# Second mixture of experts, slot 0: which engine forms the six low parts of the next slot's first-layer weights

## The chip, the cores and the metric

One core of one Trainium2 chip runs the kernel. The time is the device time of one execution in microseconds (us). Engines: TensorE (PE in the profile, PEld its weight loads), VectorE (DVE), ScalarE (ACT), GpSimd (POOL), SyncE (SP, a DMA queue here). Times inside the profile count from the start of its span.

## The reference, cut to what matters

Three stages follow each other: a linear attention with a delta rule over 768 steps, a bilinear layer, and a mixture of experts that sends each of 3072 tokens to one of 8 experts. The change lies in the third:

```
def _moe2_ref(x, modality_id, w_gate, modality_bias, w1, w2):
    logits = x @ w_gate + modality_bias[modality_id]
    e_idx = np.argmax(logits, axis=1)
    ...
    for e in range(E):
        mask = e_idx == e
        h = np.maximum(x[mask] @ w1[e], 0.0)
        out[mask] = gate_w[mask, None] * (h @ w2[e])
```

Here D = 384 (three blocks of 128 rows, kk = 0 to 2), F = 1024, E = 8, all in float32.

## The kernel before, in words

Every product of float32 matrices is made of three passes on parts: a high part (a copy rounded to fp32r) and a low part (the value less its high part). A weight w1 thus becomes w1h and w1l, and ph = w1h*xh + w1h*xl + w1l*xh.

The experts' stage works in slots of 256 tokens that share an expert (`back`, line 1265), and two half slots. A slot has eight blocks f = 0 to 7 of 128 hidden columns. For each block TensorE writes ph (two PSUM buffers, tag AB, in turn), ScalarE makes hh (the ReLU's high part) from it, and VectorE makes hl from ph and hh; the second layer (`second`) takes them two blocks later into spy or px. The ph of block f can start when the hl of block f - 2 has read its buffer.

Beside its own blocks a slot prepares the next: in each block `ahead(...)` lets the generator `weights` (line 1214) make a number of pieces of the next expert's weights, and `tokens2` (line 1241) transposes the next tokens (spt, sxh, sxl). In slot 0 two pieces are made in each of blocks 0 to 2 and one in each later block. The first six pieces are those of w1: for each kk and each half of 512 columns ScalarE casts the raw tile r to w1h, and then VectorE or GpSimd subtracts to get w1l. In the weights of slot 0 itself (i = 0) VectorE makes all six; in those of the other slots VectorE makes the first W1D = 3 (W1N = 2 halves per kk, so kk = 0 and the first half of kk = 1), GpSimd the other three. The w2 pieces follow: ScalarE casts, VectorE subtracts to w2l. The raw tiles r have five buffers; a load in SP's queue waits until its buffer has been read by both the cast and the subtraction.

Slot 0 also carries the end of the routing (`late`, line 1088, and `place`, line 931), one step per block: in block 1 TensorE counts (pr) and VectorE computes pos, cnt, pos, pf, hi, hi, lo; in block 2 VectorE makes four one-hot tiles (hot); in block 4 TensorE multiplies them (pl) and VectorE adds the result to list. GpSimd's queue starts the stage with two stores of the last token rows (x2d<-xr).

The order of the work on each engine is the order in which the program issues it (a helper chains every instruction behind the one before it on its engine), so an engine never takes a later instruction first. All operations carry the line of that helper, L86, in the profile.

Of the kernel before, what the change touches and what calls it, by code (L numbers as in the profile page):

```python
# [8 lines left out]
F32 = mybir.dt.float32  # L9
# [7 lines left out]
ALU = mybir.AluOpType  # L17
# [50 lines left out]
XGB, W1D, SLAG, W1N = 3, 3, 2, 2  # L68
# [37 lines left out]
class Kernel:  # L106
# [976 lines left out]
    def moe2(self, early, cur):  # L1083
# [26 lines left out]
        def weights():  # L1110

            for j in range(1, len(kinds)):
# [3 lines left out]
                for _ in self.weights(j, todo[j], states[j]):  # L1116
                    self.done = j, self.left
                    yield

        work, self.done = weights(), (0, 0)  # L1120

        def ahead(i):
# [91 lines left out]
    def weights(self, i, fr, st):  # L1214

        nc = self.nc
        wt = self.wset[i % NSET]
        w1h = wt.tile([P, KC, DFF], F32R, tag="w1h", name="w1h")
        w1l = wt.tile([P, KC, DFF], F32R, tag="w1l", name="w1l")
        w2h = wt.tile([P, FC, DM], F32R, tag="w2h", name="w2h")  # L1220
        w2l = wt.tile([P, FC, DM], F32R, tag="w2l", name="w2l")
        st.update(w=(w1h, w1l, w2h, w2l), odd=i % 2)
        self.left = KC * W1N + FC // 2
        for kk in range(KC):
            self.at(100 + i, MIDP + MIDS * 2 * kk / 13)
            r = self.raw()
            for n, g in enumerate(range(0, DFF, DFF // W1N)):
                gs = slice(g, g + DFF // W1N)
                nc.scalar.copy(w1h[:, kk, gs], r[:, gs])
                (nc.vector if i == 0 or kk * W1N + n < W1D else nc.gpsimd).tensor_tensor(out=w1l[:, kk, gs], in0=r[:, gs], in1=w1h[:, kk, gs].bitcast(F32), op=ALU.subtract)  # L1230
                self.left -= 1
                yield
        self.at(100 + i, MIDP + MIDS * 6 / 13)
        for g in range(0, FC, 2):
            r = self.raw()
            nc.scalar.copy(w2h[:, g:g + 2], r)
            nc.vector.tensor_tensor(out=w2l[:, g:g + 2], in0=r, in1=w2h[:, g:g + 2].bitcast(F32), op=ALU.subtract)
            self.left -= 1
            yield
# [159 lines left out]
```

## Time and profile before

| | |
|---|---|
| median of 3 runs | 830.96 us (830.43 to 833.02) |
| the profiled execution | 831.49 us |
| its span | 829.8 us |
| TensorE busy | 783.9 us, 94% |
| VectorE busy | 619.0 us, 75% |
| ScalarE busy | 411.4 us, 50% |
| GpSimd busy | 169.2 us, 20% |
| mean granted TensorE clock | 0.968 of full |

The busy shares are means over all stages, so the place of the change is read by itself: slot 0 of the experts lies between about 580 and 601 us. In a timeline a row gives start, duration, engine, the operation with output and inputs, and in brackets the idle time of the engine before it and what ended it; consecutive equal operations are merged into one row with their count, which then gives the time from the first's start to the last's end. The granted clock is a share of full speed: 1.00 is 2.4 GHz, 0.50 is 1.2 GHz.

### The profile page before, as it was taken

What the parts mean: (1) busy time and instruction counts of PE and PEld (TensorE: products, weight loads), DVE (VectorE), ACT (ScalarE), POOL (GpSimd) and SP (SyncE); (2) the same over time, 40 slices, a digit from 0 to 9 for tenths busy, and PEclk for the clock granted to TensorE, in tenths of its full rate; (3) what the DMA queues carried; (4) which work ended last, traced back from release to release, by engine and by line L of the source; (5) the groups of instructions that cost most, each with busy time, mean ns of one, the idle gap of its engine ahead of it and who ended that gap; (6) DMA issues with size and microseconds to landing.
All of it is one profiled execution on the core that took longest, in us unless ns stands there. A gap on an engine that the chain in (4) does not pass through costs nothing.

```text
span 829.8 us, 23509 instructions
## 1 busy us (share of the span) xinstructions
PE 783.9 (94%) x9519; PEld 727.8 (88%) x9519; DVE 619.0 (75%) x1571; ACT 411.4 (50%) x873; POOL 169.2 (20%) x179
## 2 busy tenths in 40 slices
PE   5797689999999999999999999999999999999994
PEld 5564459899999999999999999999899999999983
DVE  5998878769767977797689864567986777677641
ACT  6366675562536254515552353334555556555541
POOL 4021203100001000010100000003254654645330
PEclk8598889999999999999999999999999999999997
DMA  9953552304121412143112300037556687667610
GB/s 299 299 176 114 159 128 98 85 23 130 44 66 33 123 44 61 39 118 71 36 53 52 102 19 25 21 124 239 172 190 230 219 264 248 220 238 239 215 54 7
DMA packets 71813, 105.35 MB, mean 127 GB/s; under 512 B 33988, under 2 KB 53332, under 8 KB 71696
## 3 DMA queue, kind: packets, MB, share of 16 engines
q1 hardware_dynamic: 64464, 88.35, 34.9%
q0 software_dynamic: 4064, 11.06, 4.0%
q10 hardware_dynamic: 3168, 4.34, 1.5%
q8 instruction: 77, 1.26, 0.7%
q14 instruction: 40, 0.33, 0.1%
HBM read 89.15 MB, written 10.63 MB: 120 GB/s over the span
## 4 chain that ended last, share of the span: by engine, by line
PE 71%; DVE 10%; issue 9%; POOL 4%; ACT 3%; DMA 2%; SPq 0%; POOLq 0%; ACTq 0%; DVEq 0%
PE pAB L86 24%; PE px L86 16%; PE ph L86 8%; PE pkq L86 4%; PE pw L86 3%; PE spy L86 3%; PE py L86 3%; PE pu L86 3%; DVE TT L86 2%; PE pS L86 2%; POOL w1l L86 2%; PE pg L86 2%; DVE tmp L86 2%; DVE Tt L86 1%; PE pf L86 1%
## 5 line engine op out<-in xcount | busy, mean ns | idle before, releaser
L86 PE MATMUL pAB<-x,w 128*128 128x256 f32 x1728 | 229.2, 287 | 0.0
L86 PEld LDWEIGHTS pAB<-x,w 128*128 128x128 f32 x1728 | 214.0, 191 | 4.4
L86 ACT CAST ch<-a 128x256 fp32r<-128x256 f32 x96 | 39.0, 406 | 120.5 <-DVE a L86 120.5
L86 ACT COPY a<-pAB 128x256 f32<-128x256 f32 x96 | 35.7, 372 | 105.2 <-PE pAB L86 97.1
L86 DVE TENSOR_TENSOR a<-a,pAB 128x256 f32<-128x256 f32 x96 | 39.9, 416 | 63.4 <-ACT a L86 62.9
L86 PE MATMUL ph<-sxh,w1h 128*128 128x256 f32 x288 | 82.2, 285 | 1.5 <-DVE hl L86 1.5
L86 PE MATMUL ph<-sxh,w1l 128*128 128x256 f32 x288 | 80.8, 281 | 0.0
L86 PE MATMUL ph<-sxl,w1h 128*128 128x256 f32 x288 | 80.7, 280 | 0.0
L86 ACT ACTIVATE hh<-ph 128x256 fp32r<-128x256 f32 x96 | 37.0, 385 | 86.1 <-PE ph L86 85.7
L86 DVE TENSOR_TENSOR Tt<-tmp,Tt 128x31 f32<-128x31 f32 (+15 forms) x186 | 66.1, 355 | 6.4
L86 DVE TENSOR_TENSOR w2l<-r,w2h 128x768 fp32r<-128x768 f32 x56 | 60.7, 1096 | 11.5 <-ACT w2h L86 11.4
L86 DVE SCALAR_TENSOR_TENSOR hl<-ph,hh 128x256 fp32r<-128x256 f32 x96 | 40.1, 418 | 37.0 <-ACT hh L86 36.6
L86 DVE TENSOR_TENSOR tmp<-Ab,Tt 128x31 f32<-128x31 f32 (+15 forms) x186 | 65.5, 352 | 3.0
L86 PE MATMUL px<-w34h,ch 128*128 128x392 f32 x192 | 65.6, 342 | 0.0
L86 PE MATMUL px<-w34h,cl 128*128 128x392 f32 x192 | 65.5, 341 | 0.0
L86 PE MATMUL px<-w34l,ch 128*128 128x392 f32 x192 | 65.4, 341 | 0.0
L86 POOL TENSOR_TENSOR w1l<-r,w1h 128x512 fp32r<-128x512 f32 x39 | 50.1, 1302 | 46.0 <-ACT w1h L86 45.9
L86 PEld LDWEIGHTS ph<-sxh,w1h 128*128 128x128 f32 x288 | 54.2, 188 | 2.7 <-DVE hl L86 2.5
L86 DVE TENSOR_TENSOR cl<-a,ch 128x256 fp32r<-128x256 f32 x96 | 40.8, 425 | 20.1 <-ACT ch L86 19.3
L86 PEld LDWEIGHTS ph<-sxh,w1l 128*128 128x128 f32 x288 | 54.3, 189 | 0.0
L86 PEld LDWEIGHTS ph<-sxl,w1h 128*128 128x128 f32 x288 | 54.2, 188 | 0.0
L86 ACT CAST w1h<-r 128x512 fp32r<-128x512 f32 x84 | 49.5, 615 | 5.9 <-DMA r<-in_e_w_dram 5.4
(263 smaller groups left out, 1676.1 us busy)
## 6 DMA issues: line engine op xcount, KB each, us to landing
r<-in_e_w_dram SPq DMA_DIRECT2D x42, 512.0 KB, 5.1
r<-in_e_w_dram SPq DMA_DIRECT2D x56, 384.0 KB, 4.2
raw<-in_w_dram SPq DMA_DIRECT2D x25, 512.0 KB, 4.1
kT<-in_kt_dram SPq DMA_DIRECT2D x12, 512.0 KB, 4.8
X<-in_q_dram SPq DMA_DIRECT2D x24, 256.0 KB, 4.5
vt<-in_v_dram SPq DMA_DIRECT2D x12, 384.0 KB, 5.3
kb<-in_kb_dram SPq DMA_DIRECT2D x12, 384.0 KB, 5.0
x2d<-xr ACTq DMA_DIRECT2D x22, 192.5 KB, 2.7
```

What stands on the lines that cost most here:

```text
L86: x = f(*a, **kw)
```

## The change

It alters the choice of engine for w1l in `weights`: the first three pieces go to VectorE only for slots after slot 1 (i > 1). For i = 1, which is prepared in slot 0, all six pieces go to GpSimd. For i = 0 all six stay on VectorE. The subtraction, its operands and the order of issue stay.

```
--- before.py
+++ after.py
@@ -1227,7 +1227,7 @@
             for n, g in enumerate(range(0, DFF, DFF // W1N)):
                 gs = slice(g, g + DFF // W1N)
                 nc.scalar.copy(w1h[:, kk, gs], r[:, gs])
-                (nc.vector if i == 0 or kk * W1N + n < W1D else nc.gpsimd).tensor_tensor(out=w1l[:, kk, gs], in0=r[:, gs], in1=w1h[:, kk, gs].bitcast(F32), op=ALU.subtract)
+                (nc.vector if i == 0 or i > 1 and kk * W1N + n < W1D else nc.gpsimd).tensor_tensor(out=w1l[:, kk, gs], in0=r[:, gs], in1=w1h[:, kk, gs].bitcast(F32), op=ALU.subtract)
                 self.left -= 1
                 yield
```

## Rows read from the trace of the kernel before

**Rows 1.** The page's first line.

```profile
span 829.8 us, 23509 instructions
```

**Rows 2.** Busy time by stretches: each engine's us (instructions), TensorE clock, DMA share, GB/s.

```profile
583.30:590.60 7.30, 5.25 (x38) 4.66 (x35) 7.13 (x17) 5.18 (x13) 5.06 (x6) 1.00 0.60 164
590.60:800.00 209.40, 208.80 (x1473) 206.54 (x1474) 153.52 (x292) 118.04 (x250) 106.04 (x91) 1.00 0.67 220
```

**Rows 3.** Waits of TensorE, 580 to 606: total, times, longest.

```profile
PE ph L86 <- DVE hl L86: 1.5, 2, 1.1
PE spt L86 <- DVE sxl L86: 0.6, 1, 0.6
```

**Rows 4.** Chain of waits in slot 0: start, us, what.

```profile
590.57 1.32 PE ph L86 x9
591.88 0.18 PE pl L86 x2
```

**Rows 5.** Timeline of VectorE in slot 0, and one row of ScalarE's.

```profile
583.67 1.28 DVE L86 TENSOR_TENSOR w1l<-r,w1h 128x512 fp32r<-128x512 f32 x2
584.88 0.42 DVE L86 SCALAR_TENSOR_TENSOR hl<-ph,hh 128x256 fp32r<-128x256 f32 x1
...
585.54 1.78 DVE L86 TENSOR_TENSOR w1l<-r,w1h 128x512 fp32r<-128x512 f32 x1
...
587.52 0.98 DVE L86 TENSOR_TENSOR pos<-pos,oh 128x16 f32<-128x16 f32 x1
...
588.74 1.04 DVE L86 TENSOR_SCALAR hi<-pf 128x2 f32<-128x2 f32 x1
...
590.09 0.42 DVE L86 SCALAR_TENSOR_TENSOR hl<-ph,hh 128x256 fp32r<-128x256 f32 x1
...
583.72 0.38 ACT L86 ACTIVATE hh<-ph 128x256 fp32r<-128x256 f32 x1
```

**Rows 6.** Timeline of GpSimd in slot 0.

```profile
583.95 1.16 POOL L86 DMA_DIRECT2D x2d<-xr  x2 [14.07 <-ACT w1h L86]
585.49 1.28 POOL L86 TENSOR_TENSOR w1l<-r,w1h 128x512 fp32r<-128x512 f32 x1 [0.38 <-ACT w1h L86]
587.12 2.59 POOL L86 TENSOR_TENSOR w1l<-r,w1h 128x512 fp32r<-128x512 f32 x2 [0.36 <-ACT w1h L86]
```

**Rows 7.** VectorE's routing operations by tile: duration in ns, min/median/max; first, last start.

```profile
L86 DVE TENSOR_TENSOR pos<-pos,oh x12: 162/163/980, 185.4 to 587.5; 128x16 f32<-128x16 f32 x12
...
L86 DVE TENSOR_SCALAR hi<-pf x12: 168/170/1036, 185.8 to 588.7; 128x2 f32<-128x2 f32 x12
...
L86 DVE TENSOR_SCALAR hot<-cols,lo,tok x24: 306/308/382, 193.8 to 591.2; 128x128 f16<-128x128 bf16 x24
```

**Rows 8.** Timelines of VectorE and GpSimd in slot 2.

```profile
628.22 3.44 DVE L86 TENSOR_TENSOR w2l<-r,w2h 128x768 fp32r<-128x768 f32 x1 [0.30 <-ACT w2h L86]
...
628.29 2.55 POOL L86 TENSOR_TENSOR w1l<-r,w1h 128x512 fp32r<-128x512 f32 x2
```

**Rows 9.** Busy time by stretches around two idle times of TensorE; columns as in rows 2.

```profile
90.91:97.37 6.46, 0.00 (x1) 0.00 (x0) 6.22 (x11) 2.55 (x6) 3.89 (x6) 0.74 0.44 128
108.99:112.41 3.42, 0.00 (x1) 0.00 (x0) 2.92 (x6) 3.04 (x7) 0.00 (x0) 0.80 0.00 0
112.41:117.87 5.46, 5.46 (x9) 2.93 (x10) 5.03 (x8) 4.19 (x8) 0.00 (x0) 0.50 0.14 27
```

**Rows 10.** Timeline of TensorE behind the second of these idle times.

```profile
112.41 5.59 PE L86 MATMUL pw<-wose,TT 128*128 128x392 f32 x8 [3.42 <-DVE TT L86]
...
118.50 2.14 PE L86 MATMUL pw<-wos,TT 128*128 128x392 f32 x6
```

**Rows 11.** SP's third load of r in slot 0, the landings (575 to 600), the cast.

```profile
589.74 0.35 SPq L86 DMA_DIRECT2D r<-in_e_w_dram  x1
...
DMA to landing us min/median/max: 3.2/3.6/4.1
...
598.73 0.61 ACT L86 CAST w1h<-r 128x512 fp32r<-128x512 f32 x1
```

More of the change, by code (lines that the diff above doesn't have):

```diff
@@ L1229, in weights @@
                 nc.scalar.copy(w1h[:, kk, gs], r[:, gs])
-                (nc.vector if i == 0 or kk * W1N + n < W1D else nc.gpsimd).tensor_tensor(out=w1l[:, kk, gs], in0=r[:, gs], in1=w1h[:, kk, gs].bitcast(F32), op=ALU.subtract)
+                (nc.vector if i == 0 or i > 1 and kk * W1N + n < W1D else nc.gpsimd).tensor_tensor(out=w1l[:, kk, gs], in0=r[:, gs], in1=w1h[:, kk, gs].bitcast(F32), op=ALU.subtract)
                 self.left -= 1
```

## The prediction

> **What bounds the kernel now.** I began with the page: the span is 829.8 us [rows 1]; the execution itself took 831.49, 0.53 above the median of the runs, 830.96, and I add the sum to 831.0. Next, the busy time by stretches: from 590.6 to 800 TensorE works 208.80 of 209.40 us at a granted clock of 1.00, while in the 7.3 us before it works only 5.25 [rows 2]. Thus slot 0 is the one place where this change can meet idle TensorE time, and what slot 0 ends later by, the end gets in full: there are 0.6 us of idle time to absorb it in the next 200. The waits of TensorE there say on whom: ph on VectorE's hl, twice, 1.5 us, the longest 1.1; spt on sxl, 0.6 [rows 3]. The chain of waits enters TensorE from that hl at 590.57, and 1.3 us later comes pl, the product of the hot tiles [rows 4]. (Blocks are f=0 to 7; the late hl is that of f=2, which frees the buffer that the ph of f=4 writes. pl stands behind this ph in TensorE's order, and everything of TensorE stands behind pl.)
>
> VectorE's timeline shows why hl is late [rows 5]: two w1l (1.28 us), hl, sxl, a third w1l that takes 1.78, then routing: pos 0.98, hi 1.04. The medians of these two are 0.163 and 0.170 [rows 7]. GpSimd's timeline beside it: the three long ones end where a GpSimd w1l ends, at about 586.77, 588.5 and 589.7 [rows 6]. So a VectorE operation with two SBUF inputs (w1l, pos), and the tensor_scalar hi, wait while GpSimd runs its subtraction; hl and sxl, which read PSUM, do not. Waiting makes 1.1 + 0.8 + 0.9 = 2.8 us, the work in the w1l 2.0.
>
> **What the change removes.** Three w1l leave VectorE, 1.28 + 1.78 = 3.06 us between the hl of f=0 and pos. Not all comes back: the hl of f=1 needs hh, written by ScalarE from 583.72 to 584.10 [rows 5]. Then hl at 584.15, sxl at 584.5, two short routing operations from 584.8, and the first held one, pos (from pos and oh), asks at about 585.15 and not 587.6. The 0.6 us wait of spt for sxl goes.
>
> **What it adds.** GpSimd has six w1l in a row. Its queue first issues the two x2d stores of the last token rows, 583.95 to 585.11 [rows 6]; by then four of six casts are done, and the fifth was there at 587.12, before its turn. A pair takes 2.59 us, so six take 7.8: GpSimd subtracts without a gap from 585.1 to 592.9, where it did so in three pieces until 589.7. Behind them in its queue stands only the fill of ids, needed much later.
>
> VectorE still has seven operations ahead of pl that I take for held ones: pos, hi, the second hi, four hot. (lo I take as free.) hi and hot are both tensor_scalar with SBUF operands; no row shows hot beside a GpSimd subtraction, its nearest row is hi, held to 1036 ns [rows 7]. The price hangs on who goes first when one GpSimd w1l ends and the next is queued. Two rows differ. pos, waiting since 587.6, got in between the second and third GpSimd w1l [rows 5, 6]. But the w2l at 628.22, queued ahead of the pair that began at 628.29, took 3.44 us: it waited for both and then needed its usual 0.9 [rows 8].
>
> Bounds: if VectorE gets in at every handover, the second hi ends near 589.0, hl (f=2) at 589.5, TensorE begins ph at 589.6, a microsecond early; but four hot then wait for the fourth, fifth and sixth w1l, the last ends at 593.15, and pl comes at 593.2, not 591.9: plus 1.3. If it never gets in, pos starts at 592.9, then pf, hi, hi, lo (four of 0.17) and hl 0.42: ph at 594.0 and not 590.57, plus 3.4; the hot then run beside ph. If hot is never held and every handover is won, TensorE resumes a microsecond early: minus 1.0. With one or two of three handovers won before 592.9, hl begins at about 593.1: plus 2.9. I take that, between the two rows.
>
> **The clock.** TensorE would then stand still from about 589.0 to 593.5, 4.5 us. The traced idle times of 3.42 and 6.46 us, both in the start, have a mean granted clock of 0.80 and 0.74: it fell from 1.00 to 0.50, from 2.4 to 1.2 GHz, 2.1 and 3.1 us into them. Behind the shorter one 5.46 us of work ran at 0.50, so that low stretch was 1.4 + 5.5 = 6.8 us [rows 9]. Eight 128x392 matmuls then take 5.59 us, 0.70 each, and six at full clock 2.14, 0.36 each [rows 10]: about half is lost. An idle time of 4.5 us would leave 4.2 to 5.5 us at low clock behind it, price 2.1 to 2.7; I take 2.3. The floor is nothing (1.1 us of idleness at 590 did not move the clock), the ceiling 3.4, half of 6.8.
>
> **What costs nothing.** The three raw tiles come free about 3 us later (the third at 592.9 and not 589.7), so their next loads do. The third load, issued at 589.74, lands 3.2 to 4.1 us after issue; from 592.9 that is 597.0 at the latest, and ScalarE reads it at 598.73 [rows 11]. Without this cover it would be up to 3 us. SP's queue issues in order, and nothing it holds meanwhile is urgent. Slot 1 reads the last w1l at 601.4, 8 us after it is done.
>
> **Sum:** 831.0 + 2.9 + 2.3 = 836.2 us, 0.6% slower.
>
> **Rivals.**
> A, VectorE gets in at every handover. For: pos; against: w2l. Plus 1.3 without a fall of the clock, 832.3; with one, behind a stall of some 2.4 us, up to 3.2 more, 835.5.
> The Trainium skill's page "SBUF — State Buffer", section "Who interferes with whom", says that whoever issues first gets the shared port pair for its whole instruction and that the other fully blocks. By that rule a VectorE operation already waiting goes ahead of the next GpSimd one, which is A; the pos row agrees and the w2l row does not.
> The page's same section says that a tensor_scalar can take both ports, so hot would be held: by it the minus 1.0 case falls away.
>
> B, the other side: routing slips through. Its operations read 2 to 192 elements; if they fit into the gaps and hot is free, hl of f=2 is done before 590.5, and the waits of 0.6 and up to 1.0 us go. It decides at the handovers of 586.4 to 589.0. Time 829.4 to 830.0. Against: pos and hi, just as short, were held 0.8 and 0.9 us.
>
> C, held as forecast, but the clock stays: 831.0 + 2.9 = 833.9, with the bound of 834.4.
>
> That the change does nothing is no case: the three VectorE w1l at 583.67 and 585.54 are those of i=1.
>
> **How the numbers follow.** Forecast (held past handovers, clock falls) 0.45, C 0.07, A with the clock's fall 0.15, A without 0.15, B 0.15, something faster that I don't see 0.03. A measurement here tells 0.3%, 2.5 us, from no change. Slower by over that: 0.45 + 0.07 + 0.15 = 0.67; the same: A without the fall and B, 0.30; faster 0.03, since all of TensorE's waiting in slot 0 is 2.05 us. The range leaves out B and the faster case: from A without the fall, less half a microsecond of spread, 831.8, to 3.4 + 2.7 with as much spread, 837.6.
>
> **What would show it.** Right: six GpSimd w1l back to back from 585.1 to 592.9; pos, hi or hot at several times 0.17 or 0.3 us; TensorE's longest wait, in front of ph (f=4) or pl, at 2.4 to 4.5 us; a granted clock of 0.5 for some microseconds behind it; nothing new after slot 1. Wrong: the held operations at their medians, gaps between the six w1l, a clock of 1.00 all through slot 0, or a wait for a load of r.

## The result, and the profile after

Eight runs of the changed kernel have a median of 837.35 us (835.25 to 838.42), eight of the kernel before 832.77. The ratio is 1.0061, with a 95% interval of 1.0051 to 1.0071: 0.6% slower, 5 us.

The page's first line after, beside [rows 1]:

```profile
span 833.4 us, 23508 instructions
```

This execution is the quickest of the eight (835.25 us), and its span is only 3.6 us longer than before's. To see where time went, it is best to measure the slot itself, from the first ph of slot 0 to the first ph of slot 1 in TensorE's timeline: before from 580.77 to 601.38, 20.61 us; after from 579.28 to 604.66, 25.38. Slot 0 became 4.8 us longer. It also began 1.5 us earlier, for a reason that has nothing to do with the change: of the stretches at half clock in the start, the last one of before [rows 9] did not occur in this execution. These are the same stretches of the kernel after, to be read beside [rows 9], with the same columns:

```profile
108.00:112.00 4.00, 1.00 (x4) 0.23 (x2) 3.50 (x6) 3.61 (x7) 0.00 (x0) 1.00 0.00 0
112.00:118.00 6.00, 5.23 (x15) 2.88 (x16) 5.90 (x10) 5.62 (x11) 0.00 (x0) 1.00 0.14 31
```

From there to the last product of the experts the two traces take 216.05 and 216.36 us, so all that slot 0 lost reached the end. TensorE's waits on ph from 576 to 800 after, to be read beside [rows 3]:

```profile
PE ph L86 <- DVE hl L86: 5.5, 2, 5.0
```

One wait of 5.0 us, before ph of f=4, stands where there was one of 1.1; the wait of spt for sxl is gone. GpSimd's and then VectorE's timeline after, beside [rows 5, 6, 7]:

```profile
582.45 1.16 POOL L86 DMA_DIRECT2D x2d<-xr  x2 [14.06 <-ACT w1h L86]
583.61 7.45 POOL L86 TENSOR_TENSOR w1l<-r,w1h 128x512 fp32r<-128x512 f32 x6
```

```profile
582.65 0.42 DVE L86 SCALAR_TENSOR_TENSOR hl<-ph,hh 128x256 fp32r<-128x256 f32 x1 [0.38 <-ACT hh L86]
...
583.60 7.50 DVE L86 TENSOR_TENSOR pos<-pos,oh 128x16 f32<-128x16 f32 x1
591.13 0.17 DVE L86 TENSOR_REDUCE pf<-pos 128x2 f32<-128x16 f32 x1
591.33 0.17 DVE L86 TENSOR_SCALAR hi<-pf 128x2 f32<-128x2 f32 x1
...
591.82 0.42 DVE L86 SCALAR_TENSOR_TENSOR hl<-ph,hh 128x256 fp32r<-128x256 f32 x1
...
592.48 0.30 DVE L86 TENSOR_SCALAR hot<-cols,lo,tok 128x128 f16<-128x128 bf16 x1
```

A multiplication of 16 numbers per partition, 0.163 us otherwise, stays in VectorE for 7.50 us: it starts with the first of six GpSimd subtractions and ends with the last, at 591.1. Behind it everything runs at its usual speed, hot too, since GpSimd is done. The chain of waits shows the price in one view:

```profile
583.68 7.42 DVE pos L86
...
591.90 0.35 DVE hl L86
592.25 0.04 issue
592.29 2.29 PE ph L86 x9
594.58 0.34 PE pl L86 x2
```

The nine matmuls of ph took 1.32 us before [rows 4] and take 2.29 here. The busy time by stretches says why (columns as in rows 2; the second stretch is TensorE's wait):

```profile
582.32:587.27 4.95, 4.95 (x34) 4.61 (x34) 4.59 (x5) 4.42 (x12) 4.82 (x5) 1.00 0.28 85
587.27:592.29 5.02, 0.01 (x1) 0.00 (x1) 4.88 (x7) 0.14 (x1) 3.83 (x5) 1.00 0.25 76
592.29:595.71 3.42, 3.42 (x14) 3.32 (x15) 3.04 (x9) 1.09 (x2) 0.00 (x0) 0.50 0.00 0
595.71:604.65 8.94, 8.94 (x61) 8.94 (x61) 7.64 (x24) 3.12 (x7) 0.00 (x0) 1.00 0.89 306
```

The granted clock fell to 0.50 as TensorE resumed, after 5.0 us of standing still, and came back 3.4 us later. Half of 3.42 is 1.7 us; the waits grew from 2.05 to 5.47, by 3.4. Together that is 5.1, for 4.8 measured in the slot. Counted by starts the sum closes: ph of f=4 comes 13.0 us into the slot and not 9.8, so 3.2 us later, and from there to slot 1 it takes 12.4 us and not 10.8, so 1.6 us more.

### The profile page after: what moved, and what is told of

Same layout as the page of the kernel before. It is cut to its first block, busy times and chain, and to the rows that moved or that the text cites. A ratio compares the mean times of both kernels' runs of the same rounds, so it can differ in the third digit from the quotient of the medians.

```text
span 833.4 us, 23508 instructions
## 1 busy us (share of the span) xinstructions
PE 783.1 (94%) x9519; PEld 727.7 (87%) x9519; DVE 621.7 (75%) x1568; ACT 411.2 (49%) x873; POOL 171.4 (21%) x182
## 4 chain that ended last, share of the span: by engine, by line
PE 70%; DVE 11%; issue 9%; POOL 4%; ACT 3%; DMA 1%; SPq 0%; POOLq 0%; ACTq 0%; DVEq 0%
PE pAB L86 25%; PE px L86 16%; PE ph L86 7%; PE pkq L86 4%; PE spy L86 3%; DVE TT L86 3%; PE py L86 3%; PE pu L86 3%; PE pw L86 2%; PE pg L86 2%; PE pS L86 2%; POOL w1l L86 2%; DVE tmp L86 1%; DVE Tt L86 1%; POOL out_dram L86 1%
## 5 line engine op out<-in xcount | busy, mean ns | idle before, releaser
L86 DVE TENSOR_TENSOR w2l<-r,w2h 128x768 fp32r<-128x768 f32 x56 | 61.9, 1117 | 12.1 <-ACT w2h L86 10.8
L86 POOL TENSOR_TENSOR w1l<-r,w1h 128x512 fp32r<-128x512 f32 x42 | 54.0, 1308 | 49.9 <-ACT w1h L86 49.4
```

The lines of the kernel that those rows point to most:

```text
L86: x = f(*a, **kw)
```

## The experiments

The theory: GpSimd's subtractions keep VectorE's routing off SBUF. The rivals: VectorE's own work is the bound, or pos waits for a signal of GpSimd's last piece. Each kernel ran beside the kernel before on the same chip. Lengths of slot 0, measured as above in one traced execution of each, with TensorE's waits in it:

| kernel | subtractions on GpSimd in slot 0 | slot 0, us | waits of TensorE, us | ratio to before, 95% |
|---|---|---|---|---|
| before | 3 | 20.61 | 0.44, 0.55, 1.05 | 1 |
| changed | 6 | 25.38 | 0.45, 5.02 | 1.0061 (1.0051 to 1.0071) |
| e1 | 0 | 19.49 | 0.44, 0.55 | 0.9989 (0.9975 to 1.0004) |
| e2 | 6, short fills between | 25.96 | 0.44, 5.44 | 1.0074 (1.0057 to 1.0091) |
| e3 | 6, TensorE kept busy | 23.95 | 0.44, 0.94 | 1.0042 (1.0026 to 1.0057) |
| e4 | 6, routing in PSUM | 23.64 | 0.46, 3.06 | 1.0031 (1.0019 to 1.0044) |
| e5 | 6, two longer fills | 25.97 | 0.45, 5.52 | 1.0069 (1.0053 to 1.0086) |
| e6 | 0, spread | 18.69 | 0.44 | 0.9975 (0.9963 to 0.9986) |
| e7 | 3, routing in PSUM | 19.99 | 0.46, 0.54, 0.54 | 0.9985 (0.9976 to 0.9994) |
| e8 | 6, three fills behind the first | 23.42 | 0.44, 0.85, 2.19 | one execution: 833.09 us, before 833.00 |
| e9 | 6, a longer fill behind each | 27.60 | 0.45, 7.38 | one execution: 839.07 us, before 833.00 |

**e1, all six on VectorE.**

```
-(nc.vector if i == 0 or kk * W1N + n < W1D else nc.gpsimd).tensor_tensor(out=w1l...
+(nc.vector if i <= 1 or kk * W1N + n < W1D else nc.gpsimd).tensor_tensor(out=w1l...
```

> All six low parts of slot 1's first layer go to VectorE, none to GpSimd. Theory (GpSimd's subtractions keep VectorE's routing out): no GpSimd operation reads in slot 0, so pos and hi fall to 0.16 and 0.17 us, a w1l takes 0.68; VectorE does 5 w1l (3.4 us) where it lost 3.06 + 1.7 us to w1l and waits before, so hl of f=2 is ready some 2 us earlier than before and TensorE's waits in slot 0 fall from 2.05 to under 1 us: 1 to 1.6 us faster than before (ratio 0.998 to 0.999), 6 us faster than the changed kernel. Rival (VectorE's own work is the bound, GpSimd's share is relief): hl of f=2 comes later by three more w1l, 2 us, and the time is 2 us above before.

Slot 0 is 1.1 us shorter than before and 5.9 shorter than changed. VectorE does twice the subtractions that it did before, and the routing is at its medians (VectorE's timeline):

```profile
585.79 1.28 DVE L86 TENSOR_TENSOR w1l<-r,w1h 128x512 fp32r<-128x512 f32 x2
...
587.28 0.17 DVE L86 TENSOR_TENSOR pos<-pos,oh 128x16 f32<-128x16 f32 x1
...
587.69 0.17 DVE L86 TENSOR_SCALAR hi<-pf 128x2 f32<-128x2 f32 x1
```

The rival of VectorE's own load falls: more work on it made the slot shorter. Over the whole kernel the ratio's interval just reaches 1, so the 0.9 us that the ratio shows is not sure by itself; what shows the gain are the slot and its waits, in the traced execution.

**e4, the routing in PSUM.** The last pos, pf and first hi live in spare columns of the PSUM tile pr.

```
+pp = self.ps.tile([P, 64], F32, tag="ps", name="pr")
+late = i == NT // MT - 1
-pos = small("pos", sh)
+pos = pp[:, 24:24 + TPU * E].rearrange(...) if late else small("pos", sh)
...
```

> The changed kernel with pos, pf and the first hi of the last token block kept in PSUM, so that these VectorE operations have at most one SBUF input. Theory (the shared SBUF reads hold them): pos 0.2 us, the first hi 0.2, ph of f=4 starts without the 5 us wait; the four hot, all SBUF, are held to the end of the GpSimd pieces, so pl comes only 0.5 to 1 us before the changed kernel's ph and TensorE waits 3 to 3.5 us there; time 1 to 2.5 us below the changed kernel, 2.5 to 4 above before. Rival 1 (hot is not held): hot at 0.3 us each, no wait over 1 us, time at or below before. Rival 2 (pos waits on a semaphore of GpSimd's last piece, not on SBUF reads): nothing changes, pos 7.5 us.

VectorE's timeline:

```profile
585.39 0.18 DVE L86 TENSOR_TENSOR pr<-pr,oh 128x16 f32<-128x16 f32 x1
...
585.82 0.17 DVE L86 TENSOR_SCALAR pr<-pr 128x2 f32<-128x2 f32 x1
...
586.22 0.16 DVE L86 SCALAR_TENSOR_TENSOR lo<-hi,pr 128x2 f32<-128x2 f32 x1
...
586.96 5.85 DVE L86 TENSOR_SCALAR hot<-cols,lo,tok 128x128 f16<-128x128 bf16 x1
592.72 0.26 DVE L86 TENSOR_SCALAR hot<-cols,hi 128x192 f16<-128x192 bf16 x1
```

In this view the tile pr stands for pos, pf and the first hi. The same two operations, pos with one SBUF input and hi with none, take 0.18 and 0.17 us in the midst of GpSimd's six (585.27 to 592.74). So pos does not wait for a signal; it waits for its second SBUF read. Nor is it the write that is held: lo, with one SBUF input, writes to SBUF beside the same subtractions in 0.16 us. For hi, which has one tensor input, the runs show only that it is held with input and output in SBUF, and not with its input in PSUM. The first hot, all in SBUF, is held instead, 5.85 us, to the same end, and TensorE waits before pl. Rival 1 falls with it: hot is held.

**e3, TensorE kept busy.** 36 matmuls more whose results are not used.

```
+if i == 0 and f == 4:
+    for _ in range(36):
+        nc.tensor.matmul(self.xt[0][:, 0:SLOT], w1h[:, 0, 0:P], xh[:, 0], start=True, stop=True)
```

> The changed kernel with 36 more 128x256 matmuls into an unused PSUM buffer between the second layer of block 1 and ph of f=4 in slot 0 (results not used, 36 x 0.117 = 4.2 us, inside the idle time of 5.0 us). Theory (the clock's fall adds to the wait): granted clock 1.00 all through slot 0, pos still held 7.5 us, TensorE idle 0.8 us, time 1.5 to 3 us below the changed kernel, some 2.5 to 3.5 above before. Rival (the low clock hid behind VectorE and costs nothing): time as the changed kernel, 5 us above before.

pos is held 7.62 us as before, and ph of f=4 starts 13.1 us into the slot, where it starts 13.0 into it in the changed kernel. What differs is the clock behind it (busy time by stretches; the first holds the added matmuls, the second starts with the remaining wait of 0.94):

```profile
588.20:592.75 4.55, 4.55 (x38) 4.34 (x37) 4.48 (x3) 0.49 (x1) 4.29 (x5) 1.00 0.26 86
592.75:596.00 3.25, 2.31 (x18) 2.27 (x18) 3.18 (x12) 0.95 (x2) 0.00 (x0) 1.00 0.00 0
596.00:604.00 8.00, 8.00 (x57) 8.00 (x56) 7.58 (x24) 3.26 (x7) 0.00 (x0) 1.00 0.78 266
```

The slot is 1.4 us shorter, and by the ratios the kernel is 1.0061 - 1.0042 = 0.19%, 1.6 us quicker (the two intervals together leave a doubt of some 1.5 us on it), with 4.4 us of useless work in it. That is the price of the clock's fall alone; the rival that it costs nothing falls, by the slot above all.

**e2, short fills.** Behind each of the six, GpSimd fills a spare 128x64 tile.

```
+if i == 1:
+    nc.gpsimd.memset(self.gap, 0.0)
```

> The changed kernel with a short GpSimd fill of a spare 128x64 tile (0.15 us, it reads nothing) behind each of the six subtractions. Theory A (VectorE is kept out only because the next reading GpSimd instruction follows without a gap): pos gets in at the first fill, so it and the two hi take at most 1.5 us each, TensorE's wait before ph (f=4) falls from 5.0 to under 1 us, the hot tiles are then held one by one and TensorE waits some 3 us before pl instead; time about 1.5 to 3 us below the changed kernel, 2 to 3.5 above before. Theory B (pos waits for the last subtraction itself, or for an empty GpSimd queue): pos takes 7.5 + 0.8 = 8.3 us and the time is 0.8 us above the changed kernel.

By its numbers this was theory B (ratio 1.0074, pos 7.93 us). But GpSimd's timeline shows that there was no gap: a fill begins before the subtraction ahead of it ends, and the next one starts 0.08 us before the fill ends.

```profile
584.57 1.33 POOL L86 TENSOR_TENSOR w1l<-r,w1h 128x512 fp32r<-128x512 f32 x1
585.79 0.19 POOL L86 MEMSET gap<- 128x64 f32 x1
585.90 1.32 POOL L86 TENSOR_TENSOR w1l<-r,w1h 128x512 fp32r<-128x512 f32 x1
```

So it did not tell the two apart. e5 used a fill of 128x512 behind the first and the third piece (`if i == 1 and n == 0 and kk < 2`).

> The changed kernel with a longer GpSimd fill of a spare 128x512 tile (0.5 to 0.6 us, it reads nothing) behind the first and behind the third of the six subtractions. In e2 a fill of 0.18 us overlapped both neighbours and left no time without a reading GpSimd instruction; pos was held past all of them. Theory A (VectorE needs a stretch in which GpSimd reads nothing): pos ends just behind the first subtraction (1.3 to 1.4 us), both hi run in the first or second gap, hl of f=2 is ready by 589.5, TensorE waits before pl and not before ph, a hot is held to the end of the last three subtractions; time 1 to 3 us below the changed kernel. Theory B (a waiting VectorE operation waits until GpSimd has no further reading instruction queued): pos takes 8.4 to 8.7 us, time 0.5 to 1.5 us above the changed kernel.

Both theories miss. VectorE's timeline:

```profile
584.51 4.32 DVE L86 TENSOR_TENSOR pos<-pos,oh 128x16 f32<-128x16 f32 x1
588.87 0.17 DVE L86 TENSOR_REDUCE pf<-pos 128x2 f32<-128x16 f32 x1
589.07 3.86 DVE L86 TENSOR_SCALAR hi<-pf 128x2 f32<-128x2 f32 x1
```

pos passed by the first gap, some 0.4 us wide at 585.9, and got in at the second, at 588.8; hi was then held behind the last three. The time stayed that of e2. Two runs more, of one execution each, asked what decides: e8 has three fills behind the first piece alone (1.7 us), e9 one behind each piece.

> The changed kernel with three GpSimd fills of the spare 128x512 tile (1.6 us together, nothing read) behind the first subtraction alone. In e5 pos passed by a gap of 0.4 us behind the first subtraction and got in at one behind the third. Theory A (the length of the gap decides): pos ends at the first gap, after 1.3 to 1.5 us; hi is held behind the other five unless it falls into the same gap, as both hi would at 0.2 us each: then hl of f=2 is ready early and only hot is held. Theory B (pos waits for every reading GpSimd instruction that was already queued when it asked, whatever lies between): pos is held past the gap, through the second and third subtraction at least (5.5 us or more).

> The changed kernel with the 128x512 fill (0.55 us) behind each of the six subtractions. Theory B (as in e8): pos ends where it did in e5, behind the third subtraction, 4.3 to 4.9 us, although there were two gaps before; hi, which asks when the last three are queued, is held until the end or close to it. Theory A (length of the gap, or chance): pos ends at the first or second gap, or passes by the third.

VectorE in e8, and GpSimd's fills and the five subtractions behind them:

```profile
583.91 1.38 DVE L86 TENSOR_TENSOR pos<-pos,oh 128x16 f32<-128x16 f32 x1
...
585.77 0.55 DVE L86 TENSOR_SCALAR hi<-hi 128x2 f32<-128x2 f32 x1
...
587.10 1.09 DVE L86 TENSOR_SCALAR hot<-cols,lo,tok 128x128 f16<-128x128 bf16 x1
588.11 1.32 DVE L86 TENSOR_SCALAR hot<-cols,hi 128x192 f16<-128x192 bf16 x1
589.36 1.29 DVE L86 TENSOR_SCALAR hot<-cols,lo,tok 128x128 f16<-128x128 bf16 x1
590.57 1.32 DVE L86 TENSOR_SCALAR hot<-cols,hi 128x192 f16<-128x192 bf16 x1
```

```profile
585.15 1.73 POOL L86 MEMSET gap<- 128x512 f32 x3
586.84 6.21 POOL L86 TENSOR_TENSOR w1l<-r,w1h 128x512 fp32r<-128x512 f32 x5
```

And VectorE in e9, with the end of GpSimd's work:

```profile
585.56 4.77 DVE L86 TENSOR_TENSOR pos<-pos,oh 128x16 f32<-128x16 f32 x1
...
590.57 5.27 DVE L86 TENSOR_SCALAR hi<-pf 128x2 f32<-128x2 f32 x1
```

```profile
594.05 1.26 POOL L86 TENSOR_TENSOR w1l<-r,w1h 128x512 fp32r<-128x512 f32 x1
595.25 0.53 POOL L86 MEMSET gap<- 128x512 f32 x1
```

In e8 pos got in at the wide gap, as A said, and then each hot got in at the very next handover, with no gap at all between five subtractions: 1.1 to 1.3 us each. In e9 pos passed two gaps and took the third, and hi passed all. Neither rule covers both. For hi, though, a fill is no gap: in e9 it ends at 595.84, behind the last fill (595.78) and not behind the last subtraction (595.31), and in e8 the second hi takes 0.55 us where GpSimd only fills. pos, which has two SBUF inputs, ended while the first fill of e8 and the third of e9 still ran. That VectorE's operations are held is shown; who wins a handover stays open.

**e6 and e7, better kernels.** e6 is e1 with one piece in blocks 0 to 2 and two in blocks 3 to 5; e7 is the kernel before with e4's PSUM routing.

```
-ahead(f - 2 * (i == 2) in (1, 2, 3), 1 + (f < 3 if i == 0 else f > 4))
+ahead(f - 2 * (i == 2) in (1, 2, 3), 1 + (2 < f < 6 if i == 0 else f > 4))
```

> As e1 (all six on VectorE), and in slot 0 one piece in blocks 0 to 2 and two in blocks 3 to 5, where e1 has two in 0 to 2. Theory (what is left of TensorE's wait in e1, 0.44 before ph and 0.55 before spt, comes from VectorE's two w1l ahead of sxl): the wait before spt goes, the 0.44 stays (it stands before the first piece); 1.3 to 2 us faster than before (ratio 0.9975 to 0.9985), 0.5 faster than e1. Rival (VectorE is only loaded later instead): a new wait of 0.5 to 2 us in blocks 4 to 7 and the time of before.

> The kernel before (three subtractions on GpSimd) with the last pos, pf and first hi in PSUM. Theory (the waits of 0.8 and 0.9 us of pos and hi made the 1.05 us wait before ph of f=4): pos and hi at 0.17 to 0.2 us, no wait before ph of f=4, a hot held up to 1 us until GpSimd's last piece ends, without effect on pl; 0.8 to 1.1 us faster than before (ratio 0.9985 to 0.999). Rival (VectorE's third w1l, held 1.1 us, is enough to keep hl late): the wait before ph stays above 0.5 us and the time is within 0.4 us of before.

e6 came out as expected, and is faster than both kernels: ratio 0.9975 to before, 2 us. Of TensorE's waits in slot 0 only the 0.4 is left; the other row lies in slot 2:

```profile
PE ph L86 <- DVE hl L86: 0.4, 1, 0.4
PE spy L86 <- DVE hl L86: 0.2, 1, 0.2
```

e7's ratio, 0.9985, is at the lower end of what was expected, though the slot gained only 0.6 us. The wait before ph of f=4 went, as the theory said, but part of it came back as a wait of spt for lo, which now reads the PSUM tile that spt needs next:

```profile
PE spt L86 <- DVE sxl L86: 0.5, 1, 0.5
PE spt L86 <- DVE lo L86: 0.5, 1, 0.5
```

## Why the prediction was right or wrong

The direction was right: 0.6% slower was forecast and 0.6% measured, and 837.35 us lies inside the range of 831.8 to 837.6, close to its end. That the total came out so well is in part luck. The base was 1.8 us too low, the wait at the handovers 0.3 to 0.5 too small, and the clock 0.6 to 0.9 too large; on the measured base the same sum would have given 838.0, beside 837.35. The step that failed is the one on the handovers (one or two of three taken as won, none of five was), and the term that was furthest off within the sum is the clock (2.3 us, measured 1.4 to 1.7).

- **What is removed, and when VectorE reaches pos.** Right. pos was to ask 2.4 us earlier, as soon as the hl of f=1 and sxl were through; it does, in the same moment as GpSimd's first subtraction starts (583.60 and 583.61). The spt wait went.
- **Six subtractions without a gap, 7.8 us.** Right: 7.45. (In before the fourth cast ended at 585.40 and not by 585.11, still ahead of its turn.)
- **What is held.** Right for pos and hi. That hl and sxl are not held could not be read from [rows 5, 6], where hl ran beside no subtraction and sxl only for its last 0.1 us; e4 shows it, with 0.42 and 0.41 us beside the six.
- **Who gets in at a handover.** The step that failed. I took one or two of three handovers as won, plus 2.9; the measured case is the bound "never gets in", plus 3.4 (the waits grew by 3.4, and ph of f=4 came 3.2 us later in the slot). Two rows of before spoke against each other, and I took the middle where the trace after has five handovers lost out of five, and e2 and e3 as many. Why pos won its one handover before and none here stays open. Rival A, to which I gave 0.30, did not happen. Nor did B.
- **hot held.** Not seen in the changed kernel, because pos was held until GpSimd had ended; e4 shows it, 5.85 us. The minus 1.0 case was rightly no part of the sum.
- **The clock.** The step was right in kind, too large in size: 2.3 forecast, 1.4 to 1.7 measured (e3 against the changed kernel; the longer way from ph of f=4 to slot 1; half of the low stretch). The sum took one length, 6.8 us, from one stretch of the start. Here TensorE stood still for 5.0 us and the clock fell only at its end, where I had it fall 2.1 to 3.1 us after the start; and the low stretch lasted 3.4 us and not 6.8. (By its own figures the estimate of 4.2 to 5.5 us should read 4.4 to 5.4.) In e2 it did fall within the wait, 2.4 us into it, and lasted 6.8 us, of which 3.76 lay behind the wait:

```profile
590.62:593.68 3.06, 0.00 (x0) 0.00 (x0) 2.92 (x7) 0.00 (x0) 1.94 (x5) 0.50 0.00 0
593.68:597.44 3.76, 3.76 (x15) 3.66 (x16) 3.33 (x10) 1.10 (x2) 0.00 (x0) 0.50 0.03 5
```

So by either course under 4 us of work ran at the low clock, and about half of that is what the fall cost. The spread of 3 us between runs of one kernel fits such differences, without being shown to come from them.

- **The base.** 831.0 came from three runs; eight runs of the kernel before give 832.77. Forecast against the base, 5.2; measured by the ratio, 5.0.
- **What costs nothing.** Right. No wait for a load of r appeared, and the rest of the kernel took as long as before.

The Trainium skill's page "SBUF — State Buffer", section "Who interferes with whom", says that an operation with two SBUF inputs contends with a GpSimd instruction that reads SBUF and blocks fully; e4 against the changed kernel agrees (0.18 and 7.50 us). The rule of the same section of the Trainium skill by which A was argued, that whoever issues first goes first, does not describe what happens among queued instructions here: pos asked before the second subtraction could run and was held past five more.

## What to carry to other kernels

Moving work from VectorE to GpSimd need not free VectorE when both read SBUF: before such a move, list the VectorE operations beside it that have two SBUF inputs or are tensor_scalar within SBUF, and price the first of them, as the bad case, as held to the end of the whole unbroken run on GpSimd, not to the end of one instruction. A short operation at the head of a chain of dependent ones is the worst to hold. Where it can't be avoided, keep that operation's operand in PSUM, or leave the work on VectorE and spread it over blocks with room, as e6 does; and look whether the wait is long enough to cost TensorE's clock as well.

## What the runs showed of the hardware

- A VectorE operation held by GpSimd isn't sure of the next turn. Lost handovers: five of five in the changed kernel, and one by w2l before [rows 8]; a gap of 0.4 us in which GpSimd only wrote was passed by in e5 and twice in e9. Won: the gap of 1.7 us in e8, and there also four handovers in a row without a gap; one by pos before. What decides was not found.
- A fill on GpSimd, which only writes, held a tensor_scalar within SBUF too (hi: 0.55 us in e8, and to the end of the last fill in e9).
- The low stretch of TensorE's clock varied: 6.8 us in the start of the kernel before and around the wait of e2, 3.4 us after the 5.0 us wait here.
- Useless matmuls made the slot 1.4 us shorter (e3 against the changed kernel), by keeping the clock at 1.00.
